# One batch's pooling moved off the accumulating loads, later attention chunks held near their place and multiplied in pairs

## The chip, the core and the metric

One core of one Trainium2 chip runs the whole program. The metric is device time in microseconds (us). All engines of the core (TensorE, called PE in the profile; VectorE, DVE; ScalarE, ACT; GpSimd, POOL; SyncE, SP, which only issues transfers) run their own instruction lists and wait for each other through semaphores.

## What is computed

The reference, cut to its core. Attention over pooled keys and values comes first, then two feed-forward layers over all 4608 tokens.

```python
# q, k, v: (8 batches, 8 heads, 576, 64), float32
k_p = k.reshape(B, H, 72, 8, D).mean(axis=3)
v_p = v.reshape(B, H, 72, 8, D).mean(axis=3)
scores = (q @ k_p.T) / sqrt(D); scores -= max(scores)
attn = exp(scores); attn /= sum(attn) + 1e-9
x = (attn @ v_p)  as  (4608 tokens, 512)
h = x @ moe_w_in                                   # 512 -> 2048
P = a0 + a1*h + a2*h^2 + a3*h^3; Q = 1 + |b0|*|h| + |b1|*h^2
x = (P / (Q + 1e-6)) @ moe_w_out                   # 2048 -> 512
h = relu(x @ moe2_w_in); out = (h*h) @ moe2_w_out
```

## The kernel before

**Feed-forward part.** Tokens are worked in 9 blocks of 512 (`TB`), blocks in four groups (`SBS`: 0-1, 2-3, 4-5, 6-8). In a group there are four phases: the two halves of the first layer's 2048 hidden features (phases 0 and 1, the rational function), then the two halves of the second layer's (phases 2 and 3, squared relu). A unit is a block in a phase; it has 8 f-tiles of 128 hidden features. For each f-tile, `mm1` makes h in PSUM with 12 products of 128x128 by 128x512, `first` and `second` make g from h (rational: five instructions on ScalarE and seven on VectorE; squared relu: three and one), and `mm2`, three f-tiles later (`LAG`), adds g times w into four PSUM banks y0 to y3 with 12 products. Every operand is a pair of a rounded high part and a low part, so each product is made of three. There are 288 f-tiles; the f-tile's number is its slot, and all other work is given a slot as its place.

**Weights.** The f-tiles' weights arrive as 1 MB of 64-bit numbers (`w_raw`), are turned by ScalarE and VectorE into the two parts (`w_decode`) in the first group, stored to scratch memory (`ws`) and loaded from there by the later groups. In `w_decode` the low part is made by VectorE, but for the f-tiles in `BY_DMA` ScalarE writes a negative copy and an accumulating transfer from GpSimd's queue adds the other term. `evac` does the same choice for x between the layers, for the blocks in `X_DMA`.

**Attention part.** The tokens are also cut in 36 chunks of 128; four chunks make a block. Per chunk there are: `q_load`, `q_split` (from chunk 9 on, parts in bf16), `qk` (products into PSUM banks called sc and xp; y0 to y3 for chunks 0 to 3), `row_max`, `exps`, `norm`, `a_turn` or `a_split` (transpose through TensorE, or through the transfer engine from chunk 9 on), `av` (products into bank xp) and `x_out` (from xp to the block's x). From chunk 9 on, `qk` makes four of the eight heads at a time, `half` 0 and then 1, each in bank sc. Chunks 0 to 3 run before the first f-tile, 4 to 7 during the first, and later chunks have places by slot (`place_chunk`): chunks 8 to 15 from slot 39 on every third slot, the later ones every fourth.

**Keys and values.** Pooling is a sum over 8 neighbouring rows. Batch 0's k is loaded whole (`kf`, four loads) and summed by VectorE (`tensor_reduce`), its v is loaded whole (`vn`, `vm`) and summed by TensorE with a matrix of ones (`sums`), both in `kv_first`. All other batches are summed by transfers: one load and seven accumulating ones from GpSimd's queue, each waiting for the one before (`k_add`, `v_add`; the source of batch 1's k is `kg`, that of its v `vt`). Batch 1 is first needed by chunk 4.

**Order.** `Plan` collects all instructions as operations with an engine, an estimated cost and dependencies; `order` runs a list schedule with due times (12 rounds, the best by its own reckoning) and `emit` issues each engine's instructions in that order. Of the operations on SP and POOL some are also held by a semaphore until an operation of a compute engine is done (`_holds`). `plan.ahead` makes the due time of an operation earlier by so many us. All instructions are therefore recorded on line 374, and tiles tell them apart.

The lines that say more than words:

```python
DEC = ((-2, "abwabwab"), (FH + LAG + 1, "bwbwbwww"), ...)   # w_raw, w_decode: first slot, buffers
BY_DMA = {(1, 1), (1, 3)}
X_DMA = (0,)
SB1_START, SB1_STEP = 39, 3
```

Of the kernel before, what the change touches and what calls it, by code (L numbers as in the profile page):

```python
# [17 lines left out]
ALU = mybir.AluOpType  # L18
# [14 lines left out]
LAG = 3  # L33
AHEAD, FIRST = 0.0, range(4)
# [10 lines left out]
BY_DMA = {(1, 1), (1, 3)}  # L45
KA, KB = 128 - SP, 2 * SP - 128
KC = SP + 2 * KB
S0W = S // 128 * (128 // POOL)
# [4 lines left out]
X_DMA = (0,)  # L53
# [71 lines left out]
class Plan:  # L125
# [9 lines left out]
    BEHIND = 0.95  # L135
    QUEUES = ("pe", "act", "dve", "pool", "sp")

    def __init__(self):
        self.ops, self.tags, self.ahead = [], {}, 0.0
# [213 lines left out]
    def order(self, rounds=12):  # L353
        self._link()
        best, rank = None, {op: op.index for op in self.ops}
        for _ in range(rounds):
            due = self._backward(rank)
            start, _ = self._run(due={op: t - op.ahead for op, t in due.items()})
# [22 lines left out]
def fused_kernel(  # L381
# [5 lines left out]
    kg: bass.AP,  # L387
# [44 lines left out]
    def dve(n, name, **kw):  # L432
        pointers = sum(isinstance(kw.get(k), View) for k in ("scalar", "scalar1"))
        plan.add("dve", 0.066 + 0.061 * pointers + n / 960, [(getattr(nc.vector, name), kw)])
# [7 lines left out]
    def pe(us, products):  # L442
        plan.add("pe", us, [(nc.tensor.matmul, p) for p in products])

    def load(n, out, in_, early=None):
        plan.add("sp", 0.6, [(nc.sync.dma_start, dict(out=out, in_=in_))], n / 360e3, early)

    def load_add(n, out, in_, early=None):
        call = nc.gpsimd.dma_start, dict(out=out, in_=in_, accum_op=ALU.add)
        plan.add("pool", 1.05, [call], n / 150e3, early)  # L450
# [102 lines left out]
    def k_add(b, r):  # L553
        n = 128 * H * SP * 4
        if b < NK:
            n, src = n // 2, kg[r].rearrange("p (g k) -> p g k", g=H // 2)
        else:
            src = kt[b - NK, :, r]
        if r == 0:
            if b >= NK:  # L560
                kp_t[b] = p1.tile([128, H, SP], F32, "kp")
            load(n, kp_t[b], src, None if b < NK else SUM_EARLY)
        else:
            load_add(n, kp_t[b], src, None if b < NK else SUM_EARLY)

    def v_add(b, r):
        n = SP * DM * 4
        if r == 0:
            if b >= NK:
                vp_t[b] = p1.tile([SP, DM], F32, "vp")  # L570
            load(n, vp_t[b], vt[b - 1, :, r], None if b < NK else SUM_EARLY)
        else:
            load_add(n, vp_t[b], vt[b - 1, :, r], None if b < NK else SUM_EARLY)

    def kv_first():


        k, v = (px.tile([128, 2, 4, TB], F32, "x").rearrange("p a b c -> p (a b c)") for _ in range(2))
        kr = k[:, 0:H // 2 * S].rearrange("p (g k r) -> p g k r", g=H // 2, r=POOL)
        vr = [v[0:min(128, S - 128 * c), TB * c:TB * (c + 1)] for c in range(5)]  # L580
        for b, t in enumerate((k, v)):
            kp_t[b] = t[:, 6 * TB:6 * TB + H // 2 * SP].rearrange("p (g k) -> p g k", g=H // 2)
            vp_t[b] = t[0:SP, 7 * TB:8 * TB]
        for g in range(H // 2):
            load(128 * S * 4, kr[:, g], kf[g].rearrange("p (k r) -> p k r", r=POOL))
            dve(S, "tensor_reduce", out=kp_t[0][:, g], in_=kr[:, g], axis=AX.X, op=ALU.add)
            if g == 0:
                q_first(0)
        act(H // 2 * SP, AF.Copy, out=kp_t[0], in_=kp_t[0], scale=SCALE)
        q_first(1)  # L590
        load(2 ** 20, v[:, 0:4 * TB], vn)
        load(2 ** 17, vr[4], vm)
        q_first(2)
        q_first(3)
        ps = ps_h.tile([128, TB], F32, "h")[0:SP]
        for c in range(5):
            n, o = min(128, S - 128 * c), S0W - 16 * c
            pe(1.0, [dict(
                out=ps, lhsT=sums[0:n, o:o + SP], rhs=vr[c], start=(c == 0), stop=(c == 4),
            )])  # L600
        act(DM, AF.Copy, out=vp_t[0], in_=ps)
# [73 lines left out]
    def qk(c, half):  # L675


        halves = (half,)
        if c < NF:
            if half:  # L680
                return
            halves = (0, 1)
        mm = []
        for a in halves:
            if c < CPB:
                ps = ps_y.tile([128, TB], F32, f"y{2 * (c % 2) + a}")
            elif a and c < NF:
# [4 lines left out]
        for hh in range(H // 2):  # L692
            for o, n, b in runs(c):
                if c < NF:
# [6 lines left out]
                    continue  # L701
                h = 2 * hh + half
                (t1, t3), (k0, k1, k2) = q_t[c], kst[b]
                for i, (l, r) in enumerate(((t1, k0), (t1, k1), (t3, k2))):
                    mm.append(dict(
                        out=sc_t[c, half][o:o + n, hh, :], lhsT=l[:, h, o:o + n], rhs=r[:, h, :],
                        start=(i == 0), stop=(i == 2),
                    ))
        pe((1.1 if c < NF else 0.46) * len(list(runs(c))), mm)
# [66 lines left out]
    def a_split(c):  # L776
# [9 lines left out]
        t = [p1.tile([128, H, CH], F16, f"at{i}") for i in range(2)]  # L786
# [4 lines left out]
    def av(c):  # L791
        q_t.pop(c)
        ps = ps_x.tile([128, TB], F32, "xp").rearrange("p (g t) -> p g t", t=CH)
        mm = []
        if c < NF:
            t = at_t.pop(c)
            for g in range(H // 2):
                for o, n, b in runs(c):
                    for par in range(2):
                        h = 2 * g + par  # L800
                        mm.append(dict(
                            out=ps[64 * par:64 * par + 64, g, o:o + n],
                            lhsT=vp_t[b][:, h * D:(h + 1) * D], rhs=t[:, 4 * par + g, o:o + n],
                            start=True, stop=True,
                        ))
            pe(1.1, mm)
            x_ps[c] = ps
            return
        t1, t2 = at_t.pop(c)
        for g in range(H // 2):  # L810
            for o, n, b in runs(c):
                v = vst[b]
                for i, (k, t) in enumerate(((128, t1), (128, t1), (KC, t2))):
                    for par in range(2):
                        h = 2 * g + par
                        mm.append(dict(
                            out=ps[64 * par:64 * par + 64, g, o:o + n],
                            lhsT=v[i][0:k, h * D:(h + 1) * D], rhs=t[0:k, 4 * par + g, o:o + n],
                            start=(i == 0), stop=(i == 2),
                        ))  # L820
        pe(0.88 + 0.3 * (len(list(runs(c))) - 1), mm)
        x_ps[c] = ps
# [13 lines left out]
    hps, gt, mid = {}, {}, {}  # L836
    yps, ysb = {}, {}

    def mm1(i, u, f):
        ps = ps_h.tile([128, TB], F32, "h")  # L840
        w, x = wt[f], xt[u[0]]
        pe(2.72, [
# [8 lines left out]
    def mm2(i, u, f):  # L851
        g, w = gt.pop(i), wt[f][:, :, TB:2 * TB]
        if f == 0:
            yps[u] = [ps_y.tile([128, TB], F32, f"y{d}") for d in range(4)]
        for d in range(4):
# [8 lines left out]
            pe(0.68, mm)  # L864

# [85 lines left out]
    def run(slot, key):  # L951
        for fn, args in todo.pop((slot, key), []):
            if args and args[0] in FIRST and fn in (k_add, v_add, k_scale, q_load, qk, row_max, exps, norm, a_turn, av, x_out):
                plan.ahead = AHEAD
            fn(*args)
            plan.ahead = 0.0

    def place_chunk(c, t):
# [3 lines left out]
        for half in range(2):  # L962
            h = 0 if CPB <= c < NF else half
# [5 lines left out]
        at(t + 6, "x", av, c)  # L969
        at(t + 7, "s", x_out, c)  # L970
# [50 lines left out]
    for i in range(-S0, N + LAG):  # L1021
# [11 lines left out]
        if m >= 0:  # L1033
# [55 lines left out]
```

## Time and profile before

| | us |
|---|---|
| median of 3 runs | 1705.56 (1703.21 to 1705.82) |
| the profiled execution's own time | 1705.07 |
| span in the profile (first to last instruction) | 1702.9 |
| PE busy | 1674.3 (98%) |
| DVE, ACT busy | 1125.0 (66%), 1110.1 (65%) |
| POOL busy | 91.2 (5%) |

The span is what the profiler sees between the first and the last instruction; 2.2 us of the execution's time lie around it. Busy shares are averages over stages that differ, so the stretches are read one by one. Matmuls overlap in the records: 12 products of 512 columns start over 2.72 us, although one lasts 0.39.

### The profile page before, as it was taken

What the parts mean: (1) busy time and instruction counts of PE and PEld (TensorE: products, weight loads), DVE (VectorE), ACT (ScalarE), POOL (GpSimd) and SP (SyncE); (2) the same over time, 40 slices, a digit from 0 to 9 for tenths busy, and PEclk for the clock granted to TensorE, in tenths of its full rate; (3) what the DMA queues carried; (4) which work ended last, traced back from release to release, by engine and by line L of the source; (5) the groups of instructions that cost most, each with busy time, mean ns of one, the idle gap of its engine ahead of it and who ended that gap; (6) DMA issues with size and microseconds to landing.
All of it is one profiled execution on the core that took longest, in us unless ns stands there. A gap on an engine that the chain in (4) does not pass through costs nothing.

```text
span 1702.9 us, 23236 instructions
## 1 busy us (share of the span) xinstructions
PE 1674.3 (98%) x8754; PEld 1363.4 (80%) x8754; DVE 1125.0 (66%) x1783; ACT 1110.1 (65%) x2256; POOL 91.2 (5%) x109
## 2 busy tenths in 40 slices
PE   6999999999999999999999999999999999999999
PEld 4777788888888888888888888888888888888887
DVE  7999997573898973344889963446988898111112
ACT  6889777796666676666567876767766665333332
POOL 2200011100000110100001101000000000000000
PEclk8999999999999999999999999999999999999999
DMA  9765389858723574936144768636105004004001
GB/s 279 170 222 158 113 262 304 265 128 263 244 75 124 122 212 87 260 88 198 50 150 118 190 153 175 182 88 222 26 1 198 1 1 175 23 1 172 26 25 50
DMA packets 106645, 238.34 MB, mean 140 GB/s; under 512 B 63684, under 2 KB 65572, under 8 KB 85796
## 3 DMA queue, kind: packets, MB, share of 16 engines
q1 hardware_dynamic: 94340, 214.10, 38.1%
q0 software_dynamic: 12192, 22.75, 8.8%
q8 instruction: 69, 1.13, 0.3%
q14 instruction: 44, 0.36, 0.1%
HBM read 176.69 MB, written 42.99 MB: 129 GB/s over the span
## 4 chain that ended last, share of the span: by engine, by line
PE 88%; DVE 5%; DMA 3%; ACT 3%; issue 1%; POOL 0%; SPq 0%; ACTq 0%; DVEq 0%; POOLq 0%
PE y L374 43%; PE h L374 42%; PE sc L374 2%; PE xp L374 2%; DVE w L374 1%; DVE p L374 1%; DVE g L374 1%; DMA x<-kg 1%; DMA x<-vt 1%; ACT v L374 1%; DVE s L374 1%; DMA wraw<-wa 1%; ACT e L374 1%; DMA ya<-wb 0%; ACT w L374 0%
## 5 line engine op out<-in xcount | busy, mean ns | idle before, releaser
L374 PE MATMUL h<-x,w 128*128 128x512 f32 x3456 | 840.0, 392 | 6.0 <-DVE p L374 4.9
L374 PEld LDWEIGHTS h<-x,w 128*128 128x128 f32 x3456 | 648.6, 189 | 145.4 <-DVE p L374 6.7
L374 PE MATMUL y<-g,w 128*128 128x512 f32 x1728 | 419.9, 391 | 2.4 <-DVE g L374 2.4
L374 PE MATMUL y<-w,g 128*128 128x512 f32 x1728 | 420.4, 392 | 0.0
L374 PEld LDWEIGHTS y<-g,w 128*128 128x128 f32 x1728 | 322.5, 188 | 70.4 <-DVE g L374 3.5
L374 PEld LDWEIGHTS y<-w,g 128*128 128x128 f32 x1728 | 321.3, 188 | 66.3 <-DVE g L374 0.3
L374 ACT ACTIVATE s<-h 128x512 f32<-128x512 f32 x288 | 171.0, 594 | 234.9 <-PE h L374 217.0
L374 DVE TENSOR_TENSOR g<-w,g 128x512 fp32r<-128x512 f32 x144 | 99.6, 691 | 329.6 <-ACT g L374 317.7
L374 ACT ACTIVATE v<-s,ln_bias 128x512 f32<-128x512 f32 x144 | 104.3, 724 | 136.1 <-DVE s L374 135.4
L374 ACT ACTIVATE g<-s 128x512 fp32r<-128x512 f32 x144 | 91.2, 633 | 103.4 <-PE y L374 102.7
L374 ACT ACTIVATE p<-h,a_sb 128x512 f32<-128x512 f32 x144 | 111.4, 773 | 17.7 <-PE h L374 14.3
L374 DVE SCALAR_TENSOR_TENSOR g<-p,a_sb,v 128x512 fp32r<-128x512 f32 x144 | 107.8, 749 | 22.2 <-ACT v L374 21.9
L374 DVE TENSOR_TENSOR p<-p,h 128x512 f32<-128x512 f32 x144 | 98.3, 683 | 26.3 <-ACT p L374 21.4
L374 DVE SCALAR_TENSOR_TENSOR s<-s,b_abs,v 128x512 f32<-128x512 f32 x144 | 107.4, 746 | 3.6 <-ACT v L374 3.5
L374 ACT ACTIVATE v<-h,b_sb 128x512 f32<-128x512 f32 x144 | 99.1, 688 | 15.8 <-DVE p L374 9.4
L374 DVE SCALAR_TENSOR_TENSOR w<-p,a_sb,w 128x512 f32<-128x512 f32 x144 | 107.6, 747 | 1.6
L374 DVE SCALAR_TENSOR_TENSOR p<-p,a_sb,h 128x512 f32<-128x512 f32 x144 | 106.9, 742 | 1.4 <-ACT v L374 1.1
L374 ACT ACTIVATE v<-v,ex_bias 128x512 f32<-128x512 f32 x144 | 103.8, 720 | 2.0
L374 DVE SCALAR_TENSOR_TENSOR w<-s,g 128x512 f32<-128x512 f32 x144 | 99.3, 689 | 3.3
L374 DVE TENSOR_TENSOR g<-w,v 128x512 fp32r<-128x512 f32 x144 | 99.0, 688 | 1.7
L374 ACT ACTIVATE w<-s 128x512 f32<-128x512 f32 x144 | 90.8, 631 | 11.4 <-DVE g L374 8.5
L374 POOL DMA_DIRECT2D kp<-kt x42 | 38.1, 908 | 627.7 <-DVE g L374 209.3
(108 smaller groups left out, 1088.5 us busy)
## 6 DMA issues: line engine op xcount, KB each, us to landing
w<-ws SPq DMA_DIRECT2D x96, 1024.0 KB, 5.7
ws<-w SPq DMA_DIRECT2D x32, 1024.0 KB, 4.9
q<-qt SPq DMA_DIRECT2D x27, 512.0 KB, 5.2
kp<-kt POOLq DMA_DIRECT2D x42, 288.0 KB, 4.9
wraw<-wb SPq DMA_DIRECT2D x8, 1024.0 KB
wraw<-wa SPq DMA_DIRECT2D x7, 1024.0 KB
yb<-wa SPq DMA_DIRECT2D x6, 1024.0 KB, 7.0
vp<-vt POOLq DMA_DIRECT2D x42, 144.0 KB, 4.8
```

The lines of the kernel that those rows point to most:

```text
L374: made = fn(**{k: v.real() if isinstance(v, View) else v for k, v in kw.items()})
```

## The change

1. Batch 1's k and v are loaded whole, like batch 0's (`kf`, `vn`, `vm` now hold both batches), into the same buffers after batch 0's sums have read them; VectorE sums k, TensorE sums v. The accumulating loads of batch 1 (seven for k, seven for v) go.
2. `AHEAD` is 5.0: the work of chunks 0 to 3, and of batch 0, counts as due 5 us earlier.
3. An operation placed at slot 16 or later, weights excepted, isn't planned before the `mm1` of the f-tile 8 slots before its place (`GATED`, `WINDOW`, `plan.after`). This is a rule for the planner; no semaphore is added for it.
4. The planner reckons slower transfers (`BEHIND`, `ADD_RATE`, `LOAD_RATE`), other VectorE costs, and tries four random variations of its due times.
5. From chunk 9 on, `qk` makes all eight heads in one go, one half in bank sc and one in xp; `av` makes two chunks in one go (`TWOS`: 13 pairs; chunk 15 stays alone), one in xp and one in sc.
6. One more f-tile's low part is made by an accumulating transfer (`BY_DMA`), and block 0's x no more (`X_DMA`).
7. The last two f-tiles' `mm2` are made output bank by output bank (`last_block`), and the result is added and stored in half tiles.

```diff
-LAG = 3
-AHEAD, FIRST = 0.0, range(4)
+LAG, TAIL = 3, 2
+BEHIND, ADD_RATE, LOAD_RATE = 1.5, 140e3, 330e3
+WINDOW, GATED = 8, 16
+SEED, TRIES = 0, 4
+AHEAD, FIRST = 5.0, range(4)
...
-BY_DMA = {(1, 1), (1, 3)}
+BY_DMA = {(1, 1), (1, 3), (1, 5)}
...
+TWOS = {c for sb in SBS for c in range(max(NF, CPB * sb[0]), CPB * sb[-1] + CPB - 1, 2)}
...
-X_DMA = (0,)
+X_DMA = ()
...
+        if self.after:
+            op.deps.add(self.after)
...
+        for n in range(rounds * tries):
+            if n % rounds == 0:
+                rank = {op: op.index for op in self.ops}
+                chance = random.Random(SEED + n)
             due = self._backward(rank)
+            apart = spread if n >= rounds else 0.0
+            start, _ = self._run(
+                due={op: t - op.ahead + chance.uniform(-apart, apart) for op, t in due.items()}
+            )
...
+        def k_sum(b):
+            for g in range(H // 2):
+                load(128 * S * 4, kr[:, g], kf[b, g].rearrange("p (k r) -> p k r", r=POOL))
+                dve(S, "tensor_reduce", out=kp_t[b][:, g], in_=kr[:, g], axis=AX.X, op=ALU.add)
...
+        def v_sum(b):
+            load(2 ** 20, v[:, 0:4 * TB], vn[b])
+            load(2 ** 17, vr[4], vm[b])
...
+            ps = ps_h.tile([128, TB], F32, "h")[0:SP]
+            for c in range(5):
...
+            act(DM, AF.Copy, out=vp_t[b], in_=ps)
+        k_sum(0)
         q_first(1)
+        v_sum(0)
+        plan.ahead = 0.0
+        k_sum(1)
+        v_sum(1)
...
+        for a in halves:
+            for hh in range(H // 2):
+                h = 2 * hh + a
+                for o, n, b in runs(c):
+                    k0, k1, k2 = kst[b]
+                    for i, (l, r) in enumerate(((t1, k0), (t1, k1), (t3, k2))):
+                        mm.append(dict(
+                            out=sc_t[c, a][o:o + n, hh, :], lhsT=l[:, h, o:o + n], rhs=r[:, h, :],
+                            start=(i == 0), stop=(i == 2),
+                        ))
...
+    def av(*cs):
+        mm, us = [], 0.0
+        for c in cs:
+            if c == cs[0]:
+                ps = ps_x.tile([128, TB], F32, "xp")
+            else:
+                ps = ps_s.tile([128, TB], F32, "sc")
...
+    def last_block(u, tiles):
+        t, _ = ysb.pop(u[0])
+        for d in range(4):
+            for i in tiles:
+                mm2(i, u, i % FH, (d,))
+            for h in range(2):
+                hh = slice(h * TB // 2, (h + 1) * TB // 2)
+                tt(TB // 2, t[d][:, hh], yps[u][d][:, hh], t[d][:, hh], ALU.add)
+                r0 = u[0] * TB + d * 128
+                load(2 ** 17, out[r0:r0 + 128, hh], t[d][:, hh])
...
+            if fn not in (w_raw, w_decode, w_fetch) and slot >= GATED:
+                plan.after = started.get(slot - WINDOW)
...
+        if c not in TWOS:
+            cs = [x for x in (c - 1, c) if x == c or x in TWOS]
+            at(t + 6, "x", av, *cs)
...
-    for r in range(POOL):
-        at(-S0, "t", k_add, 1, r)
-        at(-S0, "t", v_add, 1, r)
-    at(starts[CPB] - 1, "t", k_scale, 1)
```

## Rows read from the trace of the kernel before

**Rows 1.** The page's first part: busy time (share of the span) xinstructions.
```profile
PE 1674.3 (98%) x8754; PEld 1363.4 (80%) x8754; DVE 1125.0 (66%) x1783; ACT 1110.1 (65%) x2256; POOL 91.2 (5%) x109
```

**Rows 2.** Busy time by stretch: PE, PEld, DVE, ACT, POOL; granted clock, DMA share, GB/s.
```profile
0.00:20.00 20.00, 11.45 (x69) 7.40 (x70) 10.71 (x28) 8.89 (x31) 3.16 (x10) 1.00 0.91 302
20.00:40.00 20.00, 13.82 (x103) 9.91 (x101) 19.75 (x33) 15.95 (x34) 5.40 (x5) 0.65 0.93 277
...
178.00:253.00 75.00, 74.01 (x338) 60.79 (x337) 72.93 (x115) 58.82 (x107) 5.98 (x7) 1.00 0.59 192
400.00:800.00 400.00, 400.00 (x2222) 326.43 (x2219) 255.22 (x418) 261.67 (x577) 24.29 (x28) 1.00 0.57 160
...
20.00:178.00 158.00, 142.92 (x797) 111.84 (x796) 150.59 (x237) 136.81 (x265) 19.95 (x21) 0.92 0.65 189
```

**Rows 3.** PE's waits from 40 to 260 us: total, times, longest.
```profile
PE h L374 <- DVE p L374: 4.9, 5, 1.4
PE y L374 <- DVE g L374: 2.4, 2, 1.4
PE sc L374 <- ACT x L374: 1.6, 1, 1.6
```

**Rows 4.** PE's timeline, the first f-tiles: start, duration, work, idle before.
```profile
40.80 8.43 PE L374 MATMUL h<-x,w 128*128 128x512 f32 x24 [0.82 <-ACT x L374]
...
56.20 4.60 PE L374 MATMUL h<-x,w 128*128 128x512 f32 x12
```

**Rows 5.** PE's timeline around one half of `qk` of chunk 9.
```profile
202.71 2.88 PE L374 MATMUL y<-g,w 128*128 128x512 f32 x12
205.43 0.56 PE L374 MATMUL sc<-k,t 128*128 128x72 bf16 x12
205.83 3.01 PE L374 MATMUL h<-x,w 128*128 128x512 f32 x12
208.68 2.88 PE L374 MATMUL y<-g,w 128*128 128x512 f32 x12
```

**Rows 6.** PE's timeline around one chunk's `av`.
```profile
334.90 2.88 PE L374 MATMUL h<-x,w 128*128 128x512 f32 x12
337.71 0.88 PE L374 MATMUL xp<-at,v 128*64 128x128 f16 x24
338.52 3.02 PE L374 MATMUL y<-w,g 128*128 128x512 f32 x12
341.38 2.88 PE L374 MATMUL h<-x,w 128*128 128x512 f32 x12
```

**Rows 7.** PE by shape over the whole span: busy us, mean ns.
```profile
L374 PE MATMUL h<-x,sums 128*72 128x512 f32 x8 | 5.6, 846 | 0.0
```

**Rows 8.** DVE by shape, 20 to 178 us: busy us, mean ns, idle before.
```profile
L374 DVE TENSOR_TENSOR w<-yb,w 128x1024 fp32r<-128x1024 f32 x6 | 7.3, 1218 | 0.1
...
L374 DVE TENSOR_REDUCE mx<-sc 128x4 f32<-128x288 f32 x5 | 2.2, 440 | 0.2 <-PE xp L374 0.2
...
L374 DVE TENSOR_TENSOR q<-q,t 64x1024 f32<-64x1024 f32 x1 | 1.2, 1222 | 0.0
...
L374 DVE SCALAR_TENSOR_TENSOR kp<-kp,k 128x576 f32<-128x576 f32 x1 | 0.8, 754 | 0.0
L374 DVE TENSOR_TENSOR k<-kp,k 64x576 bf16<-64x576 f32 x1 | 0.7, 746 | 0.0
```

**Rows 9.** DVE by shape, 0 to 20 us.
```profile
L374 DVE TENSOR_REDUCE x<-x 128x72 f32<-128x576 f32 x4 | 2.9, 753 | 3.8 <-DMA x<-kf 3.8
```

**Rows 10.** Transfers issued in the first 60 us: size, median us to landing.
```profile
x<-kg POOLq DMA_DIRECT2D x7, 144.0 KB, 5.3
```

**Rows 11.** DVE's timeline at the end.
```profile
1698.33 1.37 DVE L374 TENSOR_TENSOR t<-y,t 128x512 f32<-128x512 f32 x2 [0.67 <-PE y L374]
```

**Rows 12.** PE's timeline at the end.
```profile
1696.77 2.20 PE L374 MATMUL y<-w,g 128*128 128x512 f32 x9
```

**Rows 13.** Transfers from 1690 to 1703 us, GB/s in 40 slices of 0.325 us.
```profile
GB/s 0 0 50 0 0 0 0 0 0 0 0 0 0 0 0 0 0 0 0 0 0 0 0 0 334 359 378 384 158 0 233 353 372 391 265 0 0 0 0 0
```

More of the change, by code (lines that the diff above doesn't have):

```diff
@@ L3 @@
 import math
+import random
 from contextlib import ExitStack
@@ L442, in pe @@
     def pe(us, products):
-        plan.add("pe", us, [(nc.tensor.matmul, p) for p in products])
+        return plan.add("pe", us, [(nc.tensor.matmul, p) for p in products])
     def load(n, out, in_, early=None):
-        plan.add("sp", 0.6, [(nc.sync.dma_start, dict(out=out, in_=in_))], n / 360e3, early)
+        plan.add("sp", 0.6, [(nc.sync.dma_start, dict(out=out, in_=in_))], n / LOAD_RATE, early)
     def load_add(n, out, in_, early=None):
         call = nc.gpsimd.dma_start, dict(out=out, in_=in_, accum_op=ALU.add)
-        plan.add("pool", 1.05, [call], n / 150e3, early)
+        plan.add("pool", 1.05, [call], n / ADD_RATE, early)
     def turn(out, in_):
@@ L553, in k_add @@
     def k_add(b, r):
-        n = 128 * H * SP * 4
-        if b < NK:
-            n, src = n // 2, kg[r].rearrange("p (g k) -> p g k", g=H // 2)
-        else:
[L558 to L564, printed above, removed]
+        n, src = 128 * H * SP * 4, kt[b - NK, :, r]
+        if r == 0:
+            kp_t[b] = p1.tile([128, H, SP], F32, "kp")
+            load(n, kp_t[b], src, SUM_EARLY)
+        else:
+            load_add(n, kp_t[b], src, SUM_EARLY)
     def v_add(b, r):
@@ L583, in kv_first @@
             vp_t[b] = t[0:SP, 7 * TB:8 * TB]
[L584 to L589, printed above, removed]
-        q_first(1)
[L591 to L601, printed above, removed]
+        def k_sum(b):
+            for g in range(H // 2):
+                load(128 * S * 4, kr[:, g], kf[b, g].rearrange("p (k r) -> p k r", r=POOL))
+                dve(S, "tensor_reduce", out=kp_t[b][:, g], in_=kr[:, g], axis=AX.X, op=ALU.add)
+                if b == g == 0:
+                    q_first(0)
+            k_scale(b)
+        def v_sum(b):
+            load(2 ** 20, v[:, 0:4 * TB], vn[b])
+            load(2 ** 17, vr[4], vm[b])
+            if b == 0:
+                q_first(2)
+                q_first(3)
+            ps = ps_h.tile([128, TB], F32, "h")[0:SP]
+            for c in range(5):
+                n, o = min(128, S - 128 * c), S0W - 16 * c
+                pe(1.0, [dict(
+                    out=ps, lhsT=sums[0:n, o:o + SP], rhs=vr[c], start=(c == 0), stop=(c == 4),
+                )])
+            act(DM, AF.Copy, out=vp_t[b], in_=ps)
+        k_sum(0)
+        q_first(1)
+        v_sum(0)
+        plan.ahead = 0.0
+        k_sum(1)
+        v_sum(1)
     def k_scale(b):
@@ L675, in qk @@
     def qk(c, half):
[L678 to L682, printed above, removed]
+        if half:
+            return
+        halves = (0, 1)
         mm = []
@@ L700, in qk @@
                         ))
[L701 to L709, printed above, removed]
+            pe(1.1 * len(list(runs(c))), mm)
+            return
+        t1, t3 = q_t[c]
+        for a in halves:
+            for hh in range(H // 2):
+                h = 2 * hh + a
+                for o, n, b in runs(c):
+                    k0, k1, k2 = kst[b]
[4 more added lines that the diff above has]
+                        ))
+        pe(0.1 + 0.8 * len(list(runs(c))), mm)
     def row_max(c, half):
@@ L785, in a_split @@
         dve(H * KB / 4, "tensor_copy", out=a_2[:, :, SP + KB:KC], in_=a_2[:, :, SP:SP + KB])
-        t = [p1.tile([128, H, CH], F16, f"at{i}") for i in range(2)]
+        if c in TWOS:
+            t = [p1.tile([128, H, CH], F16, f"at{i}") for i in range(2)]
+        else:
+            t = p2.tile([128, 2, H, CH], BF16, "t").bitcast(F16)
+            t = [t[:, i] for i in range(2)]
         for i, a in enumerate((a_1, a_2)):
@@ L789, in a_split @@
         at_t[c] = t
[L791 to L796, printed above, removed]
+    def av(*cs):
+        mm, us = [], 0.0
+        for c in cs:
+            q_t.pop(c)
+            if c == cs[0]:
+                ps = ps_x.tile([128, TB], F32, "xp")
+            else:
+                ps = ps_s.tile([128, TB], F32, "sc")
+            x_ps[c] = ps = ps.rearrange("p (g t) -> p g t", t=CH)
+            ts = at_t.pop(c)
+            us += 1.1 if c < NF else 0.66 * len(list(runs(c)))
@@ L808, in av @@
[L808 to L820, printed above, removed]
@@ L821, in av @@
-        pe(0.88 + 0.3 * (len(list(runs(c))) - 1), mm)
-        x_ps[c] = ps
+                    terms = ((SP, vp_t[b], ts),) if c < NF else (
+                        (128, vst[b][0], ts[0]), (128, vst[b][1], ts[0]), (KC, vst[b][2], ts[1]),
+                    )
+                    for i, (k, v, t) in enumerate(terms):
+                        for par in range(2):
+                            h = 2 * g + par
+                            mm.append(dict(
+                                out=ps[64 * par:64 * par + 64, g, o:o + n],
+                                lhsT=v[0:k, h * D:(h + 1) * D], rhs=t[0:k, 4 * par + g, o:o + n],
+                                start=(i == 0), stop=(i == len(terms) - 1),
+                            ))
@@ L824, in x_out @@
+        pe(us + (0.3 if c >= NF else 0.0), mm)
     def x_out(c):
@@ L849, in mm1, with mm2 @@
         hps[i] = ps
-    def mm2(i, u, f):
-        g, w = gt.pop(i), wt[f][:, :, TB:2 * TB]
+    def mm2(i, u, f, ds=range(4)):
+        g, w = gt[i], wt[f][:, :, TB:2 * TB]
         if f == 0:
             yps[u] = [ps_y.tile([128, TB], F32, f"y{d}") for d in range(4)]
-        for d in range(4):
+        for d in ds:
             dd = slice(d * 128, (d + 1) * 128)
@@ L954, in run @@
                 plan.ahead = AHEAD
+            if fn not in (w_raw, w_decode, w_fetch) and slot >= GATED:
+                plan.after = started.get(slot - WINDOW)
             fn(*args)
-            plan.ahead = 0.0
+            plan.ahead, plan.after = 0.0, None
     def place_chunk(c, t):
@@ L962, in place_chunk @@
         for half in range(2):
-            h = 0 if CPB <= c < NF else half
+            h = half if c < CPB else 0
             at(t + 2 + h, "s", qk, c, half)
```

65 lines of the change are left out of this document (26 added, 39 removed).

## Prediction

> **What bounds the kernel now.** The page gives PE 98% busy and no other engine more than 66% [rows 1]; that is an average, and the question is where the missing share lies and what PE does in its busy time. The table by stretch comes second. From 400 to 800 us PE has no idle at all [rows 2], and its list of waits has no entry after 260 us. There only a shorter list of products can help. From 20 to 178 us it is another kernel: DVE is busy 150.59 of 158 us and PE 142.92 [rows 2]; the first `mm1` starts at 40.80 [rows 4].
>
> Third, PE's waits between 40 and 260 us. Nearly all name DVE: 4.9 us in five waits of `mm1` for a free h bank (DVE's p reads it), and 2.4 us in two waits of `mm2` for g; 1.6 us more is the wait of chunk 4's `qk` for batch 1's pooled k [rows 3]. The first f-tiles also run at the lower clock: 24 products take 8.43 us at 40.80 and 12 take 4.60 at 56.20 [rows 4], where 12 take 2.72 (start to start) later [rows 5]. That is 3.0 + 1.9 = 4.9 us; with 4.9 + 2.4 + 1.6 = 8.9 us of waits PE loses about 14 us after its first `mm1`, and what lies before 40.8.
>
> So there are three places: the first 178 us, set by DVE; 1500 us set by PE's own list; and the end, where after PE's last product (1696.77 + 2.20 = 1698.97 [rows 12]) 3.9 us remain to the end of the span.
>
> **PE's list (part 5 of the change).** The cost of a group of attention products is read from starts, since durations overlap. In [rows 5] a y group fills 2.72 us; sc takes 205.83 - 205.43 = 0.40, and the h group behind it 208.68 - 205.83 = 2.85, 0.13 over its usual 2.72. One half of `qk` costs 0.53, two halves 1.06. In one go they are 24 products at 0.40 / 12 = 0.033 each and one return: 0.80 + 0.13 = 0.93. That is 0.13 saved for each of the 27 chunks from 9 on: 3.5 us. The three chunks that straddle two batches have twice the products and the same two returns; I give them the same.
>
> For `av` [rows 6]: the h group before it lasts 337.71 - 334.90 = 2.81 (0.09 over), its 24 products 0.81, the y group behind it 2.86 (0.14 over); 0.23 of 1.04 us is entry and return. A pair pays it once: 13 x 0.23 = 3.0 us. Does the change of output bank inside a go cost anything? `mm2` changes its bank every three products, and its 12 still start in 2.72 us [rows 5], so no. **Term: -6.5 us**, bounds 0 (each bank still pays) and -6.5; I take the whole, because the y rows are the nearest.
>
> **The first 178 us (parts 1 to 4 and 6).** DVE sets the pace, so its work is counted. *What leaves.* By their slots, chunk 8 (slot 39) and chunk 9 (42) may not be planned before slots 31 and later (some 250 us), and batch 2's split likewise; today they are worked early in the window in which DVE is full. From [rows 8]: two q subtractions at 1.22 and a copy of 0.4; k's two at 0.75 and a copy of 0.3; of chunk 8 two maxima and a sum at 0.44, one subtraction like them and two small ones, 2.1. Together 2.8 + 1.8 + 2.1 = 6.7. The extra `BY_DMA` tile saves one subtraction of 1.22: 7.9 us. Neighbours' records overlap on DVE by about a tenth, so I count 0.9 of it: 7.1 us.
>
> *What comes.* Four reductions of 0.75 us for batch 1's k [rows 9], 2.9 us. Before 20 us DVE is busy only 10.71 of 20 [rows 2], which covers them; if they land later they cost 2.9. Block 0's x now takes four subtractions (4 x 0.68 = 2.7 us, at half of [rows 11]'s pair) instead of four ScalarE copies, near 215 us: PE waited once (1.0 us) in 178 to 253, and DVE is full there too [rows 2], but works ahead on later weights, which can give way. PE gets v's five sums, 4 x 0.85 + 0.6 = 4.0 us [rows 7]. PE was busy 13.82 of 20 us from 20 to 40 [rows 2], so they have room; their price, if that cover is gone, is up to 8 us at the lower clock before the first `mm1`. The sums need a bank of the two h banks, and `mm1` of the second f-tile waits for it.
>
> *Idle that may go.* DVE idles 7.4 us in the window [rows 2]. It waits there mostly for chains that the change shortens: the first `mm1`, which was held by chunk 3 behind weight work on ACT and DVE (`AHEAD` puts chunks first), and ScalarE waiting for late weights. The accumulating chain of batch 1, seven transfers of 5.3 us one after the other [rows 10], goes, and with it chunk 4's 1.6 us. I take half of the idle, 3.5, as the range is 0 to 7.4.
>
> *What is given back.* The postponed chunks' products on PE (an estimate of 2.3 us: chunk 8's `qk` a little over an `av` of [rows 6], half of chunk 9's from [rows 5], a transpose like it) return after 253 us, where PE is full. So 7.1 + 3.5 - 2.3 = 8.3. **Term: -8.3 us**; bounds -1.9 (reductions late, no idle won: 7.1 - 2.9 - 2.3) and -13.2 (all idle, and the 1.0 us wait after 178). PE is not the limit of this: what it has to do until 178 us is 178 - 40.8 - 14 - 2.3 = 121 us, so with its first `mm1` at 36 it would be through at 157, while DVE needs until 178 - 7.1 - 3.5 = 167.
>
> *Queues.* SP loses two loads and gains six (under half a us each), POOL loses 14 issues and gains one. The second v load must wait for TensorE to have read the first; behind it on SP stand weight loads, for which ScalarE would wait. The planner's order carries that, and its slower transfers make it plan for later landings. Gated transfers get no semaphore, so an early one can only take bandwidth.
>
> **The end (part 7).** The last bank's sum is now two half instructions of about 0.4 us (0.44 for 288 columns [rows 8], 0.68 for 512 [rows 11]); they end where the one did, but the last store has 128 KB instead of 256 and no other of 256 just ahead. The 1 MB goes out in two bursts of about 370 GB/s [rows 13], so 128 KB is 0.35 us. **Term: -0.4 us**, bounds 0 and -0.7.
>
> **Sum.** -6.5 - 8.3 - 0.4 = -15.2 on the profiled execution's 1705.07 gives 1689.9; that execution is 0.5 under the median of 1705.56. I predict 1690. With the first term whole, the bounds of the other two give 1705.1 - 6.5 - 13.2 - 0.7 = 1684.7 to 1705.1 - 6.5 - 1.9 = 1696.7.
>
> **Rivals.**
> *A, only PE's list shortens.* DVE's won time is spent again in the first 178 us: batch 1's 2.3 MB come early, where the transfers are already busy 0.91 of 0 to 20 us [rows 2], weights land later, and DVE waits for them. For it: the DMA shares; against it: the accumulating transfers that go had kept those engines busy longer than plain loads of as many bytes. Time: 1705.1 - 6.9 = 1698.
> *B, the whole start is won.* DVE never idles and starts on weights in its 9.3 idle us before 20: -13 to -18 there, 1680 to 1685. Against it: DVE's instructions need ACT's results in turn.
> *C, slower: the banks.* A chunk's `qk` now takes both sc and xp, and so does a pair's `av`; until eight exponentials, or two `x_out`, have read them, nothing else may use either. If PE reaches the next group before that, it stands. Early in the kernel waits for such a bank are 1.4 us a time (the longest waits on h and y are of that size [rows 3]). Some 40 groups at 1.4 us are 56 us: 1746. It decides from 15.2 / 40 = 0.4 us a group. Against it: uses of a bank lie two and more slots of 5.4 us apart, and an exponential takes half a us, so eight take about 4. The Trainium skill's Perfetto Trace Analysis (section Matmuls) says that independent groups should rotate through PSUM banks so that emptying one overlaps the next group's products; by that rule giving both banks to one group is a loss of this kind. The trace doesn't bear it out so far, as no wait after 260 us names such a bank; by the trace the sum stays, by the rule the time would be this rival's.
> *D, slower or even by a late start.* v's sums at the lower clock (8 us) hold the second f-tile, and the idle isn't won: 1705.1 - 6.9 + 8 - 2 = 1704.
> *E, nothing.* The products cost the same in one go, and DVE's work only moves: 1705.
>
> **Chances.** Forecast (1685.5 to 1695) 54%, A (to 1699) 20%, B 13%, C 6%, D 4%, E 3%. The range 1683 to 1699 leaves out C, D, E and a part of B, about 2 in 10; the forecast's own range is 1685.5 to 1695. A difference of 0.2%, 3.4 us, is about what a measurement of this kernel can tell from no change. Forecast, A and B are faster by more: 0.87. D and E are mostly within it: 0.06. C, and what D and E have above it, is slower: 0.07.
>
> **What would show it.** Chunks from 9 on: sc and xp groups of 24 products with one 2.85 us group behind them, 13 groups of 48 for pairs, and no wait of PE after 260 us; any wait of sc or xp there speaks for C. From 20 to 178 us: no q, k or chunk 8 rows on DVE, first `mm1` before 38 us, PE's waits for DVE below 4 us; a wait of ACT or DVE for weights of several us speaks for A. At the end, 3.5 us from PE's last product to the end of the span. The prediction is wrong if the waits on DVE persist with the same sum, or new ones appear after 260 us.

## The result and the profile after

The changed kernel takes 1689.87 us (median of 4 runs, 1687.39 to 1692.98) against 1705.22 (4 runs, 1703.21 to 1705.82) for the kernel before: ratio 0.9904, 95% interval 0.9887 to 0.9921. The profiled execution took 1690.75 us with a span of 1688.7, 14.2 us shorter than before; the prediction's sum was 15.2.

The page's first part [rows 1] and the windows by stretch [rows 2]. PE's busy sum falls by 7.9 us although its list has ten products more, and POOL has fewer issues:

```profile
PE 1666.4 (99%) x8764; PEld 1365.4 (81%) x8764; DVE 1123.9 (67%) x1794; ACT 1107.5 (66%) x2254; POOL 76.6 (5%) x95
```

```profile
0.00:20.00 20.00, 10.91 (x46) 5.81 (x46) 10.18 (x28) 6.12 (x24) 1.24 (x8) 1.00 0.88 305
20.00:40.00 20.00, 17.14 (x135) 10.97 (x134) 17.82 (x32) 15.38 (x37) 0.00 (x0) 0.91 0.78 274
178.00:253.00 75.00, 74.60 (x330) 61.38 (x329) 74.67 (x113) 52.91 (x79) 9.57 (x11) 1.00 0.72 212
400.00:800.00 400.00, 400.00 (x2231) 329.92 (x2230) 256.86 (x422) 260.81 (x564) 24.05 (x28) 1.00 0.55 159
20.00:178.00 158.00, 149.42 (x828) 116.78 (x828) 153.75 (x239) 140.88 (x260) 5.42 (x6) 0.97 0.55 185
```

From 20 to 178 us DVE is busier than before, and so is PE: the same work is packed tighter, and more f-tiles fall into the window. PE's waits from 40 to 260 us [rows 3] no longer lie on one place; the list has no entry after 260:

```profile
PE xp L389 <- DVE x L389: 1.7, 1, 1.7
PE sc L389 <- DVE t L389: 1.4, 1, 1.4
PE h L389 <- DVE p L389: 1.2, 2, 0.8
PE y L389 <- ACT yb L389: 1.1, 1, 1.1
PE y L389 <- DVE g L389: 0.5, 1, 0.5
```

PE's timeline at the first f-tiles [rows 4]. The first starts 2.6 us later than before, but its 24 products take 6.56 us instead of 8.43:

```profile
43.37 6.56 PE L389 MATMUL h<-x,w 128*128 128x512 f32 x24
...
51.80 3.02 PE L389 MATMUL h<-x,w 128*128 128x512 f32 x12 [0.83 <-DVE p L389]
```

Then PE's timeline around one `qk`, now one go [rows 5], and around one pair's `av` [rows 6]:

```profile
332.30 2.20 PE L389 MATMUL y<-w,g 128*128 128x512 f32 x9
334.34 0.56 PE L389 MATMUL sc<-k,t 128*128 128x72 bf16 x12
334.74 0.56 PE L389 MATMUL xp<-k,t 128*128 128x72 bf16 x12
335.13 3.00 PE L389 MATMUL h<-x,w 128*128 128x512 f32 x12
337.96 2.88 PE L389 MATMUL y<-w,g 128*128 128x512 f32 x12
```

```profile
1068.70 2.88 PE L389 MATMUL y<-w,g 128*128 128x512 f32 x12
1071.51 0.88 PE L389 MATMUL xp<-at,v 128*64 128x128 f16 x24
1072.22 0.85 PE L389 MATMUL sc<-t,v 128*64 128x128 f16 x24
1073.01 3.02 PE L389 MATMUL h<-x,w 128*128 128x512 f32 x12
1075.86 1.52 PE L389 MATMUL y<-w,g 128*128 128x512 f32 x6
```

The 48 products of a pair cost 0.09 us ahead of them (1071.51 - 1068.70 = 2.81 over 2.72), 0.71 and 0.79 themselves, and 0.13 behind: 1.72 us. The same reckoning over all groups after 262 us (a group's time to the next feed-forward product, and what the feed-forward products beside it take over 2.72 us for twelve) gives:

| us a group | before | after | saved |
|---|---|---|---|
| `qk` of a chunk in one batch (24 chunks) | 2 x 0.527 | 0.907 | 0.147 |
| `qk` of a chunk in two batches (3) | 2 x 0.740 | 1.173 | 0.307 |
| `av` of two chunks (10 pairs) | 2 x 1.033 | 1.720 | 0.346 |
| the same with one chunk in two batches (3 pairs) | 1.033 + 1.106 | 1.793 | 0.346 |

24 x 0.147 + 3 x 0.307 + 13 x 0.346 = 8.95: **part 5 saves 9.0 us** of PE's list.

At the end [rows 11 to 13]: the timeline, then the transfers' packets and GB/s in 40 slices from 1676 to 1688.7 us:

```profile
1677.72 6.73 PE L389 MATMUL y<-w,g 128*128 128x512 f32 x29
...
1681.58 4.52 SPq L389 DMA_DIRECT2D out_dram<-t  x8
1683.81 1.43 DVE L389 TENSOR_TENSOR t<-y,t 128x256 f32<-128x256 f32 x4 [1.28 <-PE y L389]
```

```profile
GB/s 0 0 0 0 0 0 0 0 0 0 0 0 0 0 0 0 0 0 0 0 255 223 316 197 249 287 126 0 58 323 239 232 326 236 239 0 0 0 0 0
DMA packets 1152, 1.05 MB, mean 83 GB/s; under 512 B 128, under 2 KB 1152, under 8 KB 1152
```

From the start of PE's last single product (1698.58 before, 1684.07 after) to the end of the span it is 4.35 us before and 4.60 after: 0.25 us worse. By subtraction the start has to give -14.2 + 9.0 - 0.25 = -5.5 us. Marks by work done check it. PE's 6912 feed-forward products are numbered in order of start: the first begins 2.6 us later than before, the 469th (near f-tile 21) at 170.64 us instead of 177.61, the 733rd (near f-tile 32) at 231.07 instead of 238.60, which is -7.5. Behind that, up to 262 us, 1.2 us that the kernel before lost, most of it in one wait for g, are gone too; and after 262 us 3.2 us are given back: chunk 8's `qk` (1.27), its transposes (0.92) and chunk 9's two halves of `qk`, which lay at 170.11 and 205.43 us before (1.05). -7.5 - 1.2 + 3.2 = -5.5.

### The profile page after: what moved, and what is told of

It is laid out like the page before. It is cut to its first block, busy times and chain, and to the rows that moved or that the text cites. A ratio compares the mean times of both kernels' runs of the same rounds, so it can differ in the third digit from the quotient of the medians.

```text
span 1688.7 us, 23257 instructions
## 1 busy us (share of the span) xinstructions
PE 1666.4 (99%) x8764; PEld 1365.4 (81%) x8764; DVE 1123.9 (67%) x1794; ACT 1107.5 (66%) x2254; POOL 76.6 (5%) x95
## 4 chain that ended last, share of the span: by engine, by line
PE 90%; DVE 7%; ACT 1%; issue 1%; DMA 1%; SPq 0%; DVEq 0%; ACTq 0%
PE y L389 44%; PE h L389 44%; DVE w L389 2%; PE xp L389 2%; PE sc L389 1%; DVE p L389 1%; DVE g L389 1%; DVE s L389 1%; DVE ya L389 0%; DMA ya<-wa 0%; DVE yb L389 0%; DVE x L389 0%; DVE t L389 0%; DMA x<-kf 0%; ACT w L389 0%
## 5 line engine op out<-in xcount | busy, mean ns | idle before, releaser
L389 ACT ACTIVATE e<-e,sm 128x72 f32<-128x72 f32 x256 | 70.9, 347 | 7.6 <-DVE sm L389 7.5
```

Source lines behind the costliest of these rows:

```text
L389: made = fn(**{k: v.real() if isinstance(v, View) else v for k, v in kw.items()})
```

## The experiments

Each kernel is set against the kernel before on its own chip, by the ratio; the kernel before has medians of 1705.22, 1709.66, 1706.08 and 1706.02 us in the four series. The marks are the starts of the 1st, the 469th and the 733rd feed-forward product in the profiled execution, one for each kernel. The same program profiled twice (the second and third rows) differs by 1.8, 1.4 and 1.4 us in them, so differences of that size say nothing.

| kernel | median us | ratio (95%) | 1st | 469th | 733rd |
|---|---|---|---|---|---|
| before | 1705.22 | | 40.80 | 177.61 | 238.60 |
| changed | 1689.87 | 0.9904 (0.9887 to 0.9921) | 43.37 | 170.64 | 231.07 |
| changed, on a second chip | 1689.02 | 0.9903 (0.9889 to 0.9918) | 41.53 | 169.23 | 229.68 |
| chunks singly in `av` | 1694.54 | 0.9910 (0.9896 to 0.9925) | 37.27 | 169.54 | 230.38 |
| `qk` in halves | 1695.67 | 0.9916 (0.9900 to 0.9931) | 41.63 | 168.77 | 228.61 |
| `AHEAD` 0 | 1691.76 | 0.9898 (0.9883 to 0.9912) | 43.72 | 168.37 | 231.79 |
| batch 1 by accumulating loads | 1698.58 | 0.9937 (0.9920 to 0.9954) | 41.98 | 175.32 | 237.53 |
| no gate | 1689.42 | 0.9911 (0.9894 to 0.9928) | 37.91 | 167.58 | 229.64 |
| old end | 1688.29 | 0.9900 (0.9885 to 0.9915) | 39.10 | 167.96 | 228.94 |
| other random numbers | 1690.48 | 0.9914 (0.9900 to 0.9929) | 40.07 | 169.60 | 230.37 |
| batch 1's k loaded late | 1690.74 | 0.9911 (0.9893 to 0.9929) | 41.40 | 166.90 | 230.81 |
| more DVE work early | 1696.36 | 0.9946 (0.9929 to 0.9962) | 41.55 | 173.74 | 235.94 |
| the same work later | 1693.24 | 0.9928 (0.9907 to 0.9949) | 42.98 | 171.38 | 234.06 |
| before with part 5 alone | 1703.02 | 0.9977 (0.9961 to 0.9993) | 39.77 | 182.93 | 246.87 |

**Pairs undone.**

```diff
-TWOS = {c for sb in SBS for c in range(max(NF, CPB * sb[0]), CPB * sb[-1] + CPB - 1, 2)}
+TWOS = set()
```

> The changed kernel with each chunk's av alone again (no pairs). Theory: a pair saves 0.35 us (entry 0.09, drain 0.09, return 0.14 are paid once), so 13 pairs are worth 4.5 us: 1694.4 against the changed kernel's 1689.9, and after 262 us 13 more groups of 24 products with an xp of 0.81. Prediction's own price: 13 x 0.23 = 3.0 us, 1692.9. Rival (banks): pairs keep both banks busy and cost waits, so single ones are no slower: 1689.9 or less.

After 262 us the `av` groups cost 24 x 1.035 + 3 x 1.107 = 28.2 us, in the changed kernel 10 x 1.720 + 3 x 1.793 + 1.035 = 23.6: pairs are worth 4.5 us. From the 733rd product to the last it takes 1458.3 us, in the changed kernel 1453.0.

**`qk` in halves again**, a slot apart, each in sc.

```diff
-        if half:
+        if half and c < NF:
             return
-        halves = (0, 1)
+        halves = (0, 1) if c < NF else (half,)
...
-            h = half if c < CPB else 0
+            h = 0 if CPB <= c < NF else half
```

> The changed kernel with qk's two halves as two groups in bank sc again, a slot apart, from chunk 9 on. Theory: in one go a chunk saves 0.15 us and one that straddles two batches 0.31, together 24 x 0.15 + 3 x 0.31 = 4.5 us: 1694.4. Prediction's own price: 27 x 0.13 = 3.5 us, 1693.4. Rival (banks): no slower than the changed kernel, 1689.9, as nothing holds xp for qk.

The `qk` groups cost 48 x 0.527 + 6 x 0.740 = 29.7 us instead of 25.3, 4.5 more, and from the 733rd product on it takes 1458.3 us again. Both halves of the 9.0 us are borne out singly, in PE's list. The times can't settle it. By the ratios the two kernels are only 1.0 and 2.0 us longer than the changed one, within the intervals; by their own medians 4.7 and 5.8 us, but the changed kernel wasn't run beside them.

**No earlier due times for chunks 0 to 3.**

```diff
-AHEAD, FIRST = 5.0, range(4)
+AHEAD, FIRST = 0.0, range(4)
```

> The changed kernel with AHEAD 0 again: chunks 0 to 3 count as due when they are. Theory: the first mm1 is set by batch 1's early sums on VectorE and late weights, not by the due times, and VectorE sets the pace after it, so the time stays within 2 us: 1688 to 1692, the first mm1 at 41 to 45 us. Rival (the prediction): without the earlier due times the first mm1 comes 4 us or more later and the time rises by as much: 1694.

The later marks and the time are those of the changed kernel. With the other parts in place, `AHEAD` is worth nothing that can be measured.

**Batch 1 by accumulating loads again**, all other parts kept.

```diff
-        plan.ahead = 0.0
-        k_sum(1)
-        v_sum(1)
...
+    for r in range(POOL):
+        at(-S0, "t", k_add, 1, r)
+        at(-S0, "t", v_add, 1, r)
+    at(starts[CPB] - 1, "t", k_scale, 1)
```

> The changed kernel with batch 1's k and v summed by accumulating loads again. Theory: plain loads save the wait for the chain but cost VectorE three reductions ahead of chunk 0's normalisation and make the first weights late; the two are about even, 1688 to 1693, with the first mm1 at 41 us or before. Rival (the chain is the gain of the start): the 5.5 us of the start go, 1695.4, with a wait of sc for x of 1.5 us or more.

My theory fell: the first `mm1` came at 41.98 and the 733rd product 6.5 us later than in the changed kernel. By the ratio the kernel is 5.6 us longer, as the rival says, though the rival's sign, a wait of sc for x, isn't there. The changed kernel's window from 40 to 60 us, then this kernel's windows and PE's longest waits from 40 to 262 us:

```profile
40.00:60.00 20.00, 15.94 (x113) 12.15 (x110) 19.63 (x33) 18.15 (x47) 0.00 (x0) 0.89 0.51 184
```

```profile
40.00:60.00 20.00, 14.25 (x54) 10.68 (x51) 17.58 (x23) 15.83 (x21) 6.12 (x7) 0.76 0.82 239
20.00:178.00 158.00, 146.36 (x800) 115.13 (x798) 147.11 (x229) 134.13 (x250) 19.42 (x22) 0.91 0.63 188
```

```profile
PE h L389 <- DVE p L389: 6.5, 3, 3.9
PE h L389 <- ACT x L389: 1.4, 2, 0.7
```

GpSimd's timeline has the last two of the seven links for k, PE's timeline the start of chunk 4's `qk`, in the changed kernel and here:

```profile
52.95 0.89 POOL L389 DMA_DIRECT2D x<-kg  x1 [5.37 <-ACT p L389]
...
56.56 0.89 POOL L389 DMA_DIRECT2D x<-kg  x1 [1.69 <-DMA x<-kg]
```

```profile
40.17 0.34 PE L389 MATMUL sc<-x,q 64*64 64x72 f32 x2
```

```profile
66.51 0.27 PE L389 MATMUL sc<-x,q 64*64 64x72 f32 x1
```

The last link is issued at 56.56 us (47.72 in the kernel before) and lands at 64.72 (55.03), so chunk 4's `qk` starts 26 us later than in the changed kernel. Work for PE and DVE is missing from 40 to 60 us, and is done later where DVE is full: DVE is busy 147.11 of the 158 us instead of 153.75. From the first to the 733rd product PE is idle for 8.2 us here and for 4.4 in the changed kernel, and it works at the lower clock (granted 0.50) for 10.8 us against 5.2; a product starts every 0.43 us there and every 0.23 at the upper one, which makes 5.1 us lost against 2.4.

The chain isn't transfers alone. The sixth link waits 5.9 us after the fifth has landed, for an operation of ScalarE that the planner put before it. Whether a chain without such holds would do as well as the plain loads was not tried.

**No gate.**

```diff
-WINDOW, GATED = 8, 16
+WINDOW, GATED = 8, 10 ** 6
```

> The changed kernel without the gate: later chunks may be planned as early as the engines allow. Theory: chunks 8 and 9 and batch 2's split return to 100 to 180 us on VectorE, 6.7 us of it, and as VectorE sets the pace there the time rises by 3 to 6 us: 1693 to 1696, with the 21st f-tile 4 us or more later than the changed kernel's 170.6 us. Rival (the early batch-1 sums and the planner's tries are the gain of the start): within 1.5 us of the changed kernel.

My theory fell and the rival held: marks and time are as with the gate. Of the work that the theory counted only chunk 8's, 2.1 us, comes back into the window, as PE's timeline shows; there are still no rows of chunk 9's or batch 2's split on DVE from 20 to 178 us.

```profile
150.08 0.33 PE L389 MATMUL sc<-x,q 64*128 64x72 f32 x1
```

**The old end.**

```diff
-        if m == N - TAIL:
-            last_block(units[-1], range(N - TAIL, N))
-        elif 0 <= m < N - TAIL:
+        if m >= 0:
```

> The changed kernel with the last two f-tiles' mm2 in their old order and stores of whole tiles. Prediction: 0.4 us slower at the end. Theory after the trace: the bank-by-bank end buys nothing, as the last half's store leaves no earlier and eight stores of 128 KB move at a lower rate than four of 256; from the last product's start to the end of the span 4.3 to 4.4 us against 4.6 in the changed kernel, the time 0.2 us lower at most, so within the noise.

The timeline, and the transfers from 1674 to 1686.4 us:

```profile
1682.10 1.37 DVE L389 TENSOR_TENSOR t<-y,t 128x512 f32<-128x512 f32 x2 [0.67 <-PE y L389]
```

```profile
GB/s 0 0 0 0 0 0 0 0 0 0 0 0 0 0 0 0 0 0 0 0 0 0 0 0 152 396 363 383 370 27 0 337 350 397 370 238 0 0 0 0
DMA packets 576, 1.05 MB, mean 85 GB/s; under 512 B 64, under 2 KB 64, under 8 KB 576
```

From the last product to the end it is 4.10 us, half a microsecond less than the 4.60 with the new end, and less than the 4.3 to 4.4 expected: the same 1.05 MB go out in half as many packets, and faster. The kernel before has 4.35 with the same end, so the loss is 0.25 to 0.5 us. The time itself can't tell them apart.

**Other random numbers in the planner**, and **the changed kernel once more** on that chip.

```diff
-SEED, TRIES = 0, 4
+SEED, TRIES = 1000, 4
```

> The changed kernel with another seed for the planner's random variations: the same program in another order. Theory: the first mm1 moves by several us, the 21st f-tile by less than 2, and the time stays within 2 us of the changed kernel. Rival (the start's gain is a lucky order): 3 us or more slower.

> The changed kernel itself, to compare on the same chip: 0.990 to 0.991 of the kernel before.

The ratios differ by 0.0011, with overlapping intervals, the 733rd product by 0.7 us. By this one other seed, the order that was found isn't a lucky one.

**Batch 1's k loaded late.** Its loads may be planned at most 8 us ahead of their due time.

```diff
-                load(128 * S * 4, kr[:, g], kf[b, g].rearrange("p (k r) -> p k r", r=POOL))
+                load(128 * S * 4, kr[:, g], kf[b, g].rearrange("p (k r) -> p k r", r=POOL), 8.0 if b else None)
```

> Changed kernel, but batch 1's four k loads may not be planned earlier than 8 us ahead of their due time, so that its sums by VectorE no longer stand among chunk 0's work. Theory (VectorE sets the pace of the first 178 us, and a late first mm1 costs nothing): first mm1 3 to 6 us earlier than the changed kernel's 43.37 us, f-tile 21 within 2 us of the changed kernel's 170.6, time within 2 us of it (1687 to 1691). Rival (the late first mm1 is what the start lost against the prediction): f-tile 21 and the end move with the first mm1, 3 to 6 us earlier, 1684 to 1686.

DVE's timeline from 12 to 39 us shows that two of the three sums that stood among chunk 0's work have moved behind it, while one stays at 14.64:

```profile
14.64 0.74 DVE L389 TENSOR_REDUCE x<-x 128x72 f32<-128x576 f32 x1
...
30.42 0.69 DVE L389 TENSOR_REDUCE x<-x 128x72 f32<-128x576 f32 x1
...
35.71 0.74 DVE L389 TENSOR_REDUCE x<-x 128x72 f32<-128x576 f32 x1
...
37.50 0.74 DVE L389 TENSOR_REDUCE x<-x 128x72 f32<-128x576 f32 x1
```

The first `mm1` comes 2 us earlier, not 3 to 6, which is hardly more than the 1.8 between two profiles of the changed kernel. The 469th product is 3.7 us earlier, which the theory (within 2) missed and the rival has; but the 733rd is where it was, and so is the time, as the theory says. Over the nine profiles with plain loads and no added work the first `mm1` lies anywhere from 37.27 to 43.72 us, and the 469th product always from 166.9 to 170.6, without following it: 37.27 goes with 169.54, and 43.72 with 168.37.

**More DVE work, early and late.** One multiplication is done twice for six f-tiles, 6 x 0.68 = 4.1 us: the six below, or 65, 67, 70, 72, 75 and 77.

```diff
+AGAIN = {2, 5, 8, 11, 14, 17}
...
+        if i in AGAIN:
+            tt(TB, g[:, LO], w, r0, ALU.mult)
         tt(TB, g[:, LO], w, r0, ALU.mult)
```

> Changed kernel, but for f-tiles 2, 5, 8, 11, 14 and 17 the last multiplication of g's low part is done twice on VectorE, with the same result: 6 more instructions of about 0.68 us, 4.1 us of VectorE work inside the first 178 us. Theory (VectorE sets the pace there): f-tile 21 and the end 3 to 4 us later, 1692 to 1694. Rival (with batch 1's transfers gone PE's own list paces that stretch, busy 149 of 158 us): later by at most 1 us, 1689 to 1691.

> Changed kernel, but the same instruction is done twice for f-tiles 65, 67, 70, 72, 75 and 77, some 400 to 475 us in, where PE has no idle: the same 4.1 us of VectorE work in another place. Theory (PE's list alone sets the pace there): no change, within 1.5 us of the changed kernel, no wait of PE after 260 us. Rival (each instruction delays g and so mm2): up to 4 us later.

Early, the 469th product is 3.1 us later than in the changed kernel and the 733rd 4.9; the time is some 7 us longer by the ratios (0.0042), more than the 3 to 4 expected. PE's busy time from 60 to 178 us falls from 116.35 to 111.36 us. The window, then PE's longest waits from 40 to 262 us:

```profile
60.00:178.00 118.00, 111.36 (x563) 88.17 (x562) 114.17 (x172) 103.43 (x172) 8.09 (x9) 1.00 0.54 169
```

```profile
PE h L390 <- DVE p L390: 3.8, 4, 1.4
PE y L390 <- DVE g L390: 3.5, 4, 1.2
```

With 1.6 us for x, PE's waits that name DVE come to 8.9 us, against 4.8 in the changed kernel and 3.2 with the work added later: PE waits for what is added to DVE.

Late, the expectation of 1.5 us was missed too: by its ratio the kernel is about 4 us longer, though the intervals overlap. The added work isn't to blame. From the 1537th product to the 3073rd, which spans it, it takes 362.1 us, the changed kernel 361.9. The delay is there at the 733rd (3.0 us), before any added instruction, and PE, DVE and ACT work in another order from within their first 40 instructions on. So an edit anywhere can go with a start that is 3 us later; of the early kernel's 4.9 us that much may be such a shift. What both show is the direction: the added work costs time early and none where it stands later.

**Part 5 alone**, on the kernel before. Shown are its places in the order; `qk` and `av` are made as in the changed kernel.

```diff
+TWOS = {c for sb in SBS for c in range(max(NF, CPB * sb[0]), CPB * sb[-1] + CPB - 1, 2)}
...
-        at(t + 6, "x", av, c)
-        at(t + 7, "s", x_out, c)
+        if c not in TWOS:
+            cs = [x for x in (c - 1, c) if x == c or x in TWOS]
+            at(t + 6, "x", av, *cs)
+            for x in cs:
+                at(t + 7, "s", x_out, x)
...
```

> The kernel before with part 5 alone: all eight heads of a chunk in one go from chunk 9 on, chunks multiplied with v in pairs; no other part of the change. Theory (part 5 shortens PE's list by 9.0 us and touches nothing else): ratio 0.9947, 9 us under the kernel before, attention groups after 262 us 9 us cheaper, f-tile 21 and 32 where they were before (177.6 and 241.3). Rival 1 (pairs make chunk 9 due later and so also lighten the first 178 us): f-tile 21 another 2 to 3 us earlier, 11 to 12 us in all, ratio 0.993. Rival 2 (the term as predicted): 6.5 us, ratio 0.996.

The theory fell: the groups after 262 us have the changed kernel's prices (0.907, 1.173, 1.720, 1.793), so the list is shorter by the same 9.0 us, yet the median falls by 3.0 only, less than Rival 2's 6.5 too. The start has become worse: in the profiled execution, the slowest of its ten (1698.33 to 1707.27) and 4.3 us over their median, the 733rd product begins at 246.87 us, 8.3 later than before. PE also waits 2.7 us after 260 us there, for weights and g, in no case for sc or xp. GpSimd's timeline has the last link of batch 1's k; then two of PE's waits from 40 to 262 us:

```profile
56.10 0.89 POOL L375 DMA_DIRECT2D x<-kg  x1 [3.39 <-ACT yb L375]
```

```profile
PE sc L375 <- ACT x L375: 3.5, 1, 3.5
PE xp L375 <- ACT t L375: 2.3, 1, 2.3
```

The link is issued 8.4 us later than in the kernel before and lands 4.3 us later (59.35 us), and chunk 4's `qk` waits 3.5 us for the pooled k. That isn't the whole of it. Up to the 733rd product PE is idle 4.5 us longer than before, and it is at the lower clock for 18.1 us instead of 9.2, at 99.86 and at 164.71 us once more, which is another 4.2 us. Rival 1 held for the work but not for the time: chunk 9's split is gone from DVE's window, while batch 2's rows (kp, k) are still there, as in [rows 8].

## Why the prediction was nearly right

The time was, 1690 against 1689.87, but by luck: its three terms were off by 2.5, 2.8 and 0.65 us, and the errors nearly cancelled.

- **PE's list: -6.5 foretold, -9.0 measured.** The step that was mis-sized is entry and return. It took the `av` products' own 0.81 us as fixed and only 0.09 + 0.14 as the switch. The pair shows that the tail of the products belongs to the switch as well: 24 take 0.71 us when more of their kind follow and 0.79 when a feed-forward product does. That, and the ends of both groups, make 0.35 a pair instead of 0.23, and chunks in two batches save 0.31 instead of 0.13. That a change of output bank costs nothing inside a go was right.
- **The first 178 us: -8.3 foretold, -5.5 measured.** What was named as the sign came true: no q, kp or chunk 8 row on DVE, PE's waits for DVE 1.7 + 1.4 + 1.2 + 0.5 = 4.8 us instead of 7.3 (under 4 was foretold). But the cause wasn't the gate, nor, by itself, the work that left DVE. With batch 1 by accumulating loads the same rows are gone from DVE, and the 733rd product is only 1.1 us earlier than before. Without the gate the time is the same, chunk 9 leaves the window by part 5 alone, and batch 2's split is there in the kernel with part 5 alone and gone in each that has either the gate or the plain loads; which of the other edits moves it wasn't settled. DVE's idle time from 20 to 178 us fell by 3.2 us, near the 3.5 counted.

  The gain comes from the step that the prediction counted only as 1.6 us and a share of that idle: the accumulating chain. With it the 733rd product begins at 237.5 us or later (three kernels), without it at 228.6 to 231.8 (nine profiles without added work). What is given back is 3.2 us instead of 2.3. How the chain costs that much the prediction did not have: chunk 4 comes late, PE stands idle and then works at the lower clock, which takes about 4.3 us up to the 733rd product before, 5.1 with batch 1 by accumulating loads and 2.4 in the changed kernel.

  Two things stay open. The plain loads alone, on the kernel before, were not tried. And the other parts aren't worthless where the chain stays: part 5 alone gives 0.9977 and all parts but the plain loads 0.9937, 6.8 us better; which of them does it isn't known.
- **The first `mm1` before 38 us: wrong, and of no weight.** It came at 43.37, in part because three of batch 1's sums stand on DVE among chunk 0's work, at 14.28, 16.04 and 17.87 us. `AHEAD` does nothing, and with k loaded late it came at 41.40, in the changed kernel's second profile at 41.53. DVE, not the first `mm1`, sets when the 469th product comes; the early DVE work bears that out.
- **The end: -0.4 foretold, +0.25 measured.** The step took eight stores of 128 KB to move at the 370 GB/s of four of 256. They move mostly at 200 to 330, in packets half as large, and 4.25 us lie behind PE's last product, where 3.5 were foretold. The Trainium skill (Perfetto Trace Analysis, DMA Optimizations) holds both that larger transfers use the bandwidth better, small ones under 2 KB carrying an overhead each, and that splitting may let some start sooner; the packet counts and the 0.25 to 0.5 us lost side with the first here.
- **The rivals.** C fell: PE waits for no bank after 260 us in the changed kernel, though both banks go to one group. The Trainium skill (Perfetto Trace Analysis, Matmuls) would have independent groups rotate through the banks; not doing so costs nothing here, where their uses lie slots apart. B's whole start and E fell by the marks, D in that its late first `mm1` did occur and cost nothing. A fell too: the start did give 5.5 us, and its sign, long waits for weights, is weaker than before: from 20 to 178 us ScalarE waits 2.6 us for them instead of 7.1, and late weights show on PE only as 1.1 us for yb. Parts 4 (but for the seed) and 6 were not tried by themselves.

## What to carry to other kernels

Price a group of products that breaks into a stream of another kind by whole groups, from the stream before to the stream after: the switch includes the tail of the group itself, and merging two groups saves all of it. A chain of accumulating transfers is to be judged by when its last link lands and by what may start only then, the time that PE then works at the lower clock included, not by the wait that the profile puts down to it. An edit that wins where one engine's list is the limit can lose it again in a start that other engines pace, so it is to be tried alone as well as taken out. Where one engine paces a stretch, mark its middle and its end by the items of work done, since the first item's start can move by 6 us and change nothing.

## What was not expected of the hardware

- Twelve f32 products of 512 columns run in 2.72 us, but the twelve beside a `qk` take 2.83 and those behind an `av` 2.85; the f16 products themselves end 0.08 us later ahead of f32 products than ahead of their own kind.
- Seven accumulating transfers of 144 KB, 5.3 us each to landing [rows 10], took 47.72 - 11.35 = 36.4 us from the first issue to the last in the kernel before and 56.10 - 9.72 = 46.4 with part 5 alone: 6 to 8 us a link, as single links took up to 9.8 us to land, and some were held after that for an operation of another engine.
- From 20 to 40 us the granted clock was 0.91 in the changed kernel with PE busy 17.14 us, and 0.65 before with 13.82 [rows 2]; batch 1's v sums are part of the added work, and the first 24 f-tile products took 6.56 instead of 8.43 us. The clock's levels are 1.2 and 2.4 GHz; at the upper one 24 take 2 x 2.72 = 5.44 us, so a part of either went at the lower. With batch 1 by accumulating loads, without those sums, the same window has 0.66 with PE busy 15.76 us. The added products came with a higher clock: the first 24 f-tile products started 2.6 us later and ended 0.7 us later (49.93 against 49.23 us).
